# Wider zero matmuls in fewer instructions, some of them in a bank that is free

## The chip, the cores and the metric

One core of a Trainium2 chip. The time is that of one launch on the device, in microseconds (us). A ratio is the mean time of one kernel's fast runs over that of the other's of the same rounds, so not quite the ratio of the medians quoted beside it.

## The reference, cut to what matters

A recurrent attention (retention with a decay per head: 4 batches, 8 heads, 768 positions, head size 64), then a feed-forward layer on its output, all in float32:

```python
state = gamma * state + einsum('bhd,bhe->bhde', k[:, :, t], v[:, :, t])
y[:, :, t] = scale * einsum('bhd,bhde->bhe', q[:, :, t], state)
...
h = x @ w_in          # 3072 x 512 times 512 x 2048
g = h - np.tanh(h)
out = g @ w_out
```

The weights arrive as float64; the kernel loads them as raw words and converts them itself, tile by tile.

## The kernel before

The attention goes in chunks of 128 positions. A bank is here the tile that a product of TensorE is written to; the program frees it when another engine has read it (the zeros ahead of `t4` wait 1.47 us for VectorE before they may write theirs). Long before the last chunk is done, the up and down products of the feed-forward layer begin. The opening is scheduled by hand, in a string of pieces, each a letter and a number. What this document needs of them, for chunk n:

- `L` loads k, q and v; `t` and `T` transpose k and q on TensorE, `c` and `C` copy these out on ScalarE.
- `p` makes the products of chunk n, `m` masks them and `z` takes the state on VectorE; the bank is free after `z`.
- `b` and `r` are the first and second half of the outputs (into `y`), `e` a small read by ScalarE between them, `y` the copy of the output to `xT`, the input of the feed-forward layer.
- For weight tile n: `W` loads it, `A` begins its conversion on ScalarE, `D` goes on on VectorE, `G` ends it, mostly on GpSimd.
- `u` and `v` are the two halves of up product n; `x` asks for zeros.

```python
    idle = [0]

    def keep_busy(at):
        for _ in range(idle[0]):
            nc.tensor.matmul(at, busy, busy, start=True, stop=True, skip_group_check=True)
        idle[0] = 0
...
    order = """
    L0 x8 t0 c0 s0 x5 T0 w0 L1 C0 x3 t1 W0 p0 c1 s1 m0 x2 T1 z0 W1 C1 w1 x3 b0 p1 e0 A0 r0
    m1 z1 y0 A1 D0 L2 x4 b1 t2 e1 c2 G0 r1 s2 y1 D1 x3 T2 w2 L3 u0 C2 W2 p2 G1 s3 t3 m2 T3
    w3 c3 v0 z2 C3 b2 A2 L4 p3 e2 W3 D2 a0 r2 s4 y2 w4 q0 W4 m3 z3 G2 x9 t4 b3 A3 d0 T4 e3
    C4 r3 g0 L5 y3 x1 p4 A4 W5 u2 D3 s5 v2 W6 w5 m4 D4 u1 G3 a2 q2 z4 L6 x6 t5 d2 G4 T5 A5
    ...
    """
```

`busy` is a 128 x 128 tile of zeros. `x9 t4` notes nine zeros, and `t4` then writes them into its own bank before its transposes: TensorE is to have work while it waits; the aim is that its clock stays up.

## Time and profile before

| | us |
|---|---|
| median of the first 3 runs | 755.27 (754.33 to 755.91) |
| profiled span | 752.6 |
| TensorE busy | 739.6 |
| TensorE idle before 50 us / from 50 to 740 / after 740 | 7.2 / 1.6 / 4.2 |

The lines are in the prediction; one more of the timeline of TensorE, the zeros ahead of `t5` (start, length, instruction, records, and in brackets how long the engine had been idle and for whom):

```profile
43.56 1.58 PE L212 MATMUL kqTp<-busy 128*128 128x128 f32 x12 [0.31 <-DVE state L327]
```

From here to the end of the span are 709.0 us. TensorE is idle for 5.8 us of them, 4.2 of these after 740 us.

### The profile page before, as it was taken

How to read it: one execution, taken by the hardware profiler on the slowest of the kernel's cores; microseconds unless marked ns; L12 is line 12 of the kernel's file. 1: busy time of each engine (PE TensorE's matmuls, PEld its weight loads, DVE VectorE, ACT ScalarE, POOL GpSimd, SP SyncE). 2: the span in 40 equal slices, each digit the busy share in tenths (PEclk: the TensorE clock that was granted, in tenths of full speed). 3: DMA queues.
4: the chain of work that ended last, by engine and by line, in shares of the span. 5: the costliest groups of instructions: out<-in, count | busy, mean ns of one | idle time of the engine just before them, and what ended most of it. 6: DMA issues, size and time to landing. Idle time of an engine off the chain costs nothing.

```text
span 752.6 us, 13801 instructions
## 1 busy us (share of the span) xinstructions
PE 739.6 (98%) x5470; PEld 501.9 (67%) x5470; DVE 518.7 (69%) x807; ACT 389.1 (52%) x725; POOL 125.9 (17%) x108
## 2 busy tenths in 40 slices
PE   7899999999999999999999999999999999999997
PEld 7786666666667676766676666666666666666663
DVE  4899889998898666656565656555665566556653
ACT  3667486666665545445545545444344434433441
POOL 0564445435453111100111100000000000000000
PEclk9999999999999999999999999999999999999999
DMA  9982546556553353332442422000000000000000
GB/s 191 231 204 59 127 99 180 149 148 160 149 128 91 92 140 115 88 82 78 106 99 74 96 57 58 28 1 1 29 0 1 28 1 0 29 0 1 28 2 28
DMA packets 125392, 59.76 MB, mean 79 GB/s; under 512 B 109840, under 2 KB 118160, under 8 KB 125328
## 3 DMA queue, kind: packets, MB, share of 16 engines
q1 hardware_dynamic: 125184, 58.73, 30.5%
q8 instruction: 43, 0.70, 0.4%
q10 hardware_dynamic: 144, 0.15, 0.1%
q14 instruction: 21, 0.17, 0.1%
HBM read 35.80 MB, written 14.68 MB: 67 GB/s over the span
## 4 chain that ended last, share of the span: by engine, by line
PE 94%; DVE 2%; DMA 1%; SPq 1%; ACT 1%; issue 1%; DVEq 0%; ACTq 0%
PE h L414 43%; PE o L462 43%; PE y L352 3%; PE s L298 2%; PE s L304 1%; DMA raws<-in_moe_w_in_dram 1%; PE kqTp L250 1%; DMA k<-in_k_dram 1%; SPq L229 1%; PE kqTp L212 0%; DVE head L185 0%; PE y L212 0%; SPq L154 0%; DVE head L183 0%; DVE g L453 0%
## 5 line engine op out<-in xcount | busy, mean ns | idle before, releaser
L414 PE MATMUL h<-xT,w 128*128 128x256 f32 x1536 | 349.9, 381 | 0.3 <-DVE w L199 0.3
L462 PE MATMUL o<-w,g 128*128 128x512 f32 x768 | 345.6, 593 | 1.4 <-DVE sum L471 0.9
L414 PEld LDWEIGHTS h<-xT,w 128*128 128x128 f32 x1536 | 289.7, 190 | 71.1 <-issue 34.0
L462 PEld LDWEIGHTS o<-w,g 128*128 128x128 f32 x768 | 145.4, 190 | 145.7 <-issue 136.6
L423 ACT ACTIVATE u<-h 128x512 f32<-128x512 f32 x96 | 57.3, 597 | 292.0 <-PE h L414 291.9
L439 DVE TENSOR_TENSOR th<-h,th 128x512 f32<-128x512 f32 x96 | 66.3, 690 | 176.0 <-ACT th L424 175.9
L453 DVE COPY_PREDICATED g<-large,th 128x512 f32<-128x512 int32 x96 | 72.1, 751 | 10.6 <-ACT apart L273 0.5
L442 DVE SCALAR_TENSOR_TENSOR h<-q,h 128x512 f32<-128x512 f32 x96 | 66.9, 696 | 10.4 <-DVE h L440 0.5
L448 DVE SCALAR_TENSOR_TENSOR h<-q,h 128x512 f32<-128x512 f32 x96 | 66.8, 696 | 9.9
L431 ACT ACTIVATE q<-u,tab 128x512 f32<-128x512 f32 x96 | 69.4, 723 | 0.0
L432 ACT ACTIVATE q<-u,tab 128x512 f32<-128x512 f32 x96 | 69.0, 718 | 0.0
L433 ACT ACTIVATE large<-u,tab 128x512 f32<-128x512 f32 x96 | 68.7, 716 | 0.0
L452 DVE TENSOR_TENSOR g<-h,u 128x512 f32<-128x512 f32 x96 | 66.3, 691 | 3.3
L440 DVE SCALAR_TENSOR_TENSOR h<-u,h 128x512 f32<-128x512 f32 x96 | 65.8, 685 | 0.0
L424 ACT ACTIVATE th<-h 128x512 f32<-128x512 f32 x96 | 56.8, 591 | 0.0
L236 POOL TENSOR_TENSOR q<-q,tab 128x512 f32<-128x512 f32 x22 | 23.2, 1057 | 199.7 <-DMA q<-in_q_dram 113.5
L195 POOL TENSOR_TENSOR low<-low,power 128x512 f32<-128x512 f32 x30 | 38.7, 1290 | 102.2 <-DVE power L187 80.6
L199 POOL TENSOR_TENSOR w<-low,head 128x512 f32<-128x512 f32 x30 | 38.5, 1284 | 2.4
L352 PEld LDWEIGHTS y<-a,v 64*64 64x64 f32 x768 | 15.8, 134 | 17.2 <-ACT large L433 10.6
L236 POOL TENSOR_TENSOR v<-v,tab 128x512 f32<-128x512 f32 x22 | 26.5, 1206 | 0.2 <-DMA v<-in_v_dram 0.2
L352 PE MATMUL y<-a,v 64*64 64x64 f32 x768 | 21.1, 224 | 2.3 <-issue 1.8
L382 ACT COPY seen<-y 64x1 f32<-64x1 f32 x96 | 10.1, 154 | 25.3 <-PE y L352 24.9
(49 smaller groups left out, 374.4 us busy)
## 6 DMA issues: line engine op xcount, KB each, us to landing
rows<-apart SPq DMA_DIRECT2D x16, 512.0 KB, 2.6
k<-in_k_dram SPq DMA_DIRECT2D x24, 256.0 KB, 4.0
q<-in_q_dram SPq DMA_DIRECT2D x24, 256.0 KB, 4.9
v<-in_v_dram SPq DMA_DIRECT2D x24, 256.0 KB, 5.3
raw<-in_moe_w_out_dram SPq DMA_DIRECT2D x12, 512.0 KB, 3.5
out_dram<-sum SPq DMA_DIRECT2D x24, 256.0 KB, 2.0
raw<-in_moe_w_in_dram SPq DMA_DIRECT2D x14, 256.0 KB, 4.2
raw<-in_moe_w_in_dram SPq DMA_DIRECT2D x28, 128.0 KB, 3.9
```

The source lines that it names most:

```text
L352: nc.tensor.matmul(y[ds(D * col, D), r, p // 2, ts(a, D)], lhsT, rhs, start=start, stop=True, skip_group_check=True)
L414: nc.tensor.matmul(hp, w1[:, c, ts(2 * m2 + i, P)], xT[n // 2][:, c, ts(n % 2, TH)], start=(i == 0 and c == 0), stop=(c == NC - 1), skip_g ...
L431: nc.scalar.activation(q0, u, AF.Square, bias=bias0)
L432: nc.scalar.activation(q1, u, AF.Square, bias=bias1, scale=math.sqrt(A))
L433: nc.scalar.activation(large, u, AF.Relu, bias=bias_m)
L439: nc.vector.tensor_tensor(th, hp, th, op=ALU.subtract)
L440: nc.vector.scalar_tensor_tensor(hp, in0=u, scalar=R, in1=hp, op0=ALU.subtract, op1=ALU.mult, reverse0=True)
L442: nc.vector.scalar_tensor_tensor(hp, in0=q0, scalar=C0, in1=hp, op0=ALU.add, op1=ALU.mult)
L448: nc.vector.scalar_tensor_tensor(hp, in0=q1, scalar=A * C1, in1=hp, op0=ALU.add, op1=ALU.mult)
L452: nc.vector.tensor_tensor(flat, hp, u, op=ALU.mult)
L453: nc.vector.copy_predicated(flat, large.bitcast(I32), th)
L462: nc.tensor.matmul(o_p[j], gT[n, m2][:, i, ts(j, P)], w2[:, 2 * m2 + i], start=(first and i == 0), stop=(last and i == 1))
```

## The change

The intent: the same number of zero columns in fewer, wider instructions, up to a bank of 512, and in three places a bank of the up product that is free (`X`), so that the zeros need not wait until the bank of the work behind them is released.

```diff
     def keep_busy(at):
-        for _ in range(idle[0]):
-            nc.tensor.matmul(at, busy, busy, start=True, stop=True, skip_group_check=True)
-        idle[0] = 0
+        most = at.shape[-1] // P
+        while idle[0]:
+            n = min(idle[0], most)
+            zeros = busy[:, None, :].to_broadcast([P, n, P])
+            nc.tensor.matmul(at[:, : n * P].rearrange("p (n t) -> p n t", n=n), busy, zeros,
+                             start=True, stop=True, skip_group_check=True)
+            idle[0] -= n
...
-        keep_busy(tp[:, :P])
+        keep_busy(tp)
...
-        keep_busy(y[:, 0, 0])
...
+        "X": lambda n: (idle.__setitem__(0, n), keep_busy(bank("h", "zeros"))),
...
-    ... C1 w1 x3 b0 ... L2 x4 b1 ... G2 x9 t4 ...
+    ... C1 w1 X3 b0 ... L2 X4 b1 ... G2 X12 t4 ...
```

The other calls of `keep_busy` get their whole bank in the same way.

More of the change, by code (lines that the diff above doesn't have):

```diff
@@ L291, in products @@
         sp = banks("t", f"s_{ci}")
-        keep_busy(sp[:, 0, :P])
+        keep_busy(sp[:, 0])
         scores[ci] = halves = sp.rearrange("p r (w n t) -> p r w n t", w=2, n=NP)
@@ L411, in up @@
         hp = hps[n, m2][:, ts(i, TH)]
-        keep_busy(hp[:, :P])
+        keep_busy(hp)
         for c in range(NC):
@@ L459, in down @@
             o_p[j] = bank("o", f"o_{n}_{m2}_{j}")
-            keep_busy(o_p[j][:, :P])
+            keep_busy(o_p[j])
         for i in range(2):
@@ L547 @@
     order = """
-    L0 x8 t0 c0 s0 x5 T0 w0 L1 C0 x3 t1 W0 p0 c1 s1 m0 x2 T1 z0 W1 C1 w1 x3 b0 p1 e0 A0 r0
-    m1 z1 y0 A1 D0 L2 x4 b1 t2 e1 c2 G0 r1 s2 y1 D1 x3 T2 w2 L3 u0 C2 W2 p2 G1 s3 t3 m2 T3
-    w3 c3 v0 z2 C3 b2 A2 L4 p3 e2 W3 D2 a0 r2 s4 y2 w4 q0 W4 m3 z3 G2 x9 t4 b3 A3 d0 T4 e3
+    L0 x8 t0 c0 s0 x5 T0 w0 L1 C0 x3 t1 W0 p0 c1 s1 m0 x2 T1 z0 W1 C1 w1 X3 b0 p1 e0 A0 r0
+    m1 z1 y0 A1 D0 L2 X4 b1 t2 e1 c2 G0 r1 s2 y1 D1 x3 T2 w2 L3 u0 C2 W2 p2 G1 s3 t3 m2 T3
+    w3 c3 v0 z2 C3 b2 A2 L4 p3 e2 W3 D2 a0 r2 s4 y2 w4 q0 W4 m3 z3 G2 X12 t4 b3 A3 d0 T4 e3
     C4 r3 g0 L5 y3 x1 p4 A4 W5 u2 D3 s5 v2 W6 w5 m4 D4 u1 G3 a2 q2 z4 L6 x6 t5 d2 G4 T5 A5
```

## The prediction

> **What bounds the kernel now.** I read the page first: busy shares, the slices, the chain that ended last.
>
> ```profile
> PE 739.6 (98%) x5470; PEld 501.9 (67%) x5470; DVE 518.7 (69%) x807; ACT 389.1 (52%) x725; POOL 125.9 (17%) x108
> ...
> PE   7899999999999999999999999999999999999997
> ...
> PE 94%; DVE 2%; DMA 1%; SPq 1%; ACT 1%; issue 1%; DVEq 0%; ACTq 0%
> ```
>
> TensorE is busy for 739.6 of 752.6 us: all idle time together is 13.0 us, 1.7% of the span. No change that only fills or removes idle time can reach 2% (15.1 us). The low slices are the first two and the last. The table of windows says where the 13 us lie: 1.6, 2.5, 1.1 and 1.7 us in the first four stretches of 10 us, 0.3 in the fifth, none from 50 to 120, 1.6 from 120 to 740, and 4.2 after 740. The change touches only pieces before about 61 us, so the waits of TensorE in the opening matter:
>
> ```profile
> PE y L352 <- issue: 1.8, 1, 1.8
> PE kqTp L212 <- DVE state L327: 1.8, 2, 1.5
> PE kqTp L212 <- DVE busy L101: 1.1, 1, 1.1
> ...
> PE y L212 <- ACT xT L393: 0.7, 1, 0.7
> PE s L212 <- ACT kqT L262: 0.6, 1, 0.6
> ...
> PE y L352 <- ACT seen L382: 0.5, 1, 0.5
> PE h L414 <- DVE w L199: 0.3, 1, 0.3
> ```
>
> L212 is the matmul of zeros. Two of these waits stand ahead of zeros that themselves need nothing but a place to write: `y` (0.7) and `kqTp` (1.5 of the 1.8). Then the timeline of TensorE (start, length, records):
>
> ```profile
> 1.05 3.70 PE L212 MATMUL kqTp<-busy 128*128 128x128 f32 x16 [1.05 <-DVE busy L101]
> ...
> 13.42 0.28 PE L352 MATMUL y<-a,v 64*64 64x64 f32 x4
> 15.48 0.45 PE L352 MATMUL y<-a,v 64*64 64x64 f32 x12 [1.78 <-issue]
> 16.61 1.16 PE L212 MATMUL y<-busy 128*128 128x128 f32 x8 [0.68 <-ACT xT L393]
> ...
> 25.19 1.99 PE L414 MATMUL h<-xT,w 128*128 128x256 f32 x8 [0.34 <-DVE w L199]
> ...
> 30.67 2.25 PE L212 MATMUL kqTp<-busy 128*128 128x128 f32 x18 [1.47 <-DVE state L327]
> ...
> 35.26 0.46 PE L352 MATMUL y<-a,v 64*64 64x64 f32 x16 [0.46 <-ACT seen L382]
> 36.30 0.49 PE L212 MATMUL s<-busy 128*128 128x128 f32 x2 [0.57 <-ACT kqT L262]
> ```
>
> A float32 matmul is two records, so x18 is nine zeros. What the reader is to see: after each place where the change can win time there is a later row in brackets where TensorE waits anyway (25.19 for VectorE's weights, 35.26 and 36.30 for ScalarE). From 43.56 us on TensorE waits no more until after 120; only time won at that point reaches the end.
>
> [...] 128 columns every 0.111 us ((0.83 - 0.275) / 5 in a group of six records), 256 every 0.216 (16 in 3.46 us at 90.33), 512 every 0.429 (8 in 3.43 us at 86.90). So four zeros of 128 cost 8 x 0.111 = 0.89 us and one of 512 costs 2 x 0.429 = 0.86. [...] The first 16 records come every 0.228 us against 0.111 later[...]; the gaps of up to 1.8 us later on did not bring the slow rate back. [...] The page of this kernel has 43 packets and 0.70 MB on such a queue, 16 KB each[...]. [...]
>
> **The change part by part.**
> (a) Wider zeros. 47 zeros (8, 5, 3, 2, 3, 4, 3, 9, 1, 6, 3) become 17 instructions of 50 units of 128 columns (12 in place of 9). Own time: 47 x 0.222 = 10.4 us before, 50 x 2 x 0.429 / 4 = 10.7 us after. No saving by itself. The zeros that remain after 43 us, x6 and x3, get cheaper by about 0.05 us together.
> (b) Fewer instructions. 30 fewer matmuls are 120 fewer instructions in the block stream. I read the unexplained 1.78 us "issue" stall at 13.7 as a block that had not arrived: a 16 KB packet is in flight from 12.7 to 14.0 while the queues are full, and about 450 instructions had gone by[...]. Ahead of that place 14 matmuls (56 instructions) go, and 12 more in the next zeros. So the second half of chunk 0's outputs (r0) gets through before the stall, ending near 13.9 rather than 15.9, and the stall falls into b1.
> (c) X4 ahead of b1, in a free bank: no wait for the copy of y0. With r0 early, that copy can start when ScalarE has done its two conversions (14.9) and end at 15.5. b1 begins near 15.6 to 15.8 rather than 17.7, a local gain of 1.9 us. But t2 needs k_2, which lands at 11.45 + 6.1 = 17.55; r1 needs ScalarE, held until 18.2 by a conversion whose weights land at 16.9; T2 needs the scaled q, which GpSimd works on from 18.71 to 19.88 because q lands at 18.6. T2 so starts at about 19.9 and not 20.41: of 1.9 us, 0.5 remain.
> (d) That 0.5 us goes through u0 to the products of chunk 2 (22.67 to 22.2), then to nothing on TensorE: v0 waits for VectorE, which is busy from 13.65 to 28.5 without a break, and starts at 25.19 again. But the load of chunk 4 waits for exactly those products (issued at 23.43), and the weights queued behind it land at 33.52 and hold ScalarE. Both move by 0.5.
> (e) X12 ahead of t4, no wait for bank t: starts at 29.2, not 30.67, and takes 3 x 0.86 = 2.57 us, not 2.09, so t4 starts at 31.8 and not 32.76: 0.95 us. Then r3 waits at 35.26 for ScalarE, which had waited until 33.52 for weights. All of the 0.95 is lost there; what counts is the 0.5 of (d).
> (f) r3, p4, the mask, VectorE's conversion, state, x6: each is released by the one before, so x6 moves from 43.56 to about 43.05.
> (g) X3 ahead of b0: the zeros there did not wait before. 0.
> Sum on the path: 0.5 + 0.05, about 0.6 us. The order of the compiled program has the waits I expect: none on the three new groups, the wait for the copy on b1, the wait for VectorE on t4, and no new wait for the up product's bank (three extra turns of that pool could have made u2 wait for VectorE's last step on u0).
>
> **Rivals.**
> A: everything won arrives: 1.9 + 0.95 us, and perhaps 0.6 at the s bank, about 3 us, 752.3. For it: TensorE is on the chain 94% of the time. Against: the waits at 25.19, 35.26 and 36.30, each for another engine or a landing.
> B: nothing arrives, 755.3: if the early weights land no earlier because the DMA engines are full (DMA share 0.9 to 1.1 through the first 40 us), or VectorE's conversion, slowed while GpSimd works beside it (1.37 us for 0.43 at 39.11), ends at the same time. Plausible; a third of my weight.
> C: the clock falls back or a new block stall appears, because the zeros run during a wait and no longer after it[...]: 1 to 4 us slower, 757 to 759. Against: gaps stay under 2 us[...].
>
> **Range and chances.** Of 755.27, 0.6 us off is 754.7. The three runs of before spread over 1.6 us, as much as the whole effect, and B or a larger part of A move it by 1 us either way: 753.5 to 755.9. With 13 us idle in all, 2% faster is practically shut out; 2% slower would need a throttled stretch of 30 us at half rate.
>
> **What would show it.** Right: the stall of kind "issue" appears later in the program, among the y matmuls of chunk 1, or is shorter; t4's zeros start near 29.2; waits for ScalarE at r3 (near 34.8) grow by some 0.4 us; the zeros after u1 (x6) start near 43.05; the work from there to the end keeps its length, 709.1 us. Wrong: x6 at 42 or earlier (then A, and the DMA landing moved more than I think), or at 43.5 or later (B); the stall at the same instruction as before would refute the block reading; zeros of 512 columns spaced more than 0.43 us, or bracketed waits ahead of the new groups, would refute (a) and (c).

Cut out of the prediction is what no trace of this case shows: rules on the spacing of matmuls, the clock and the arrival of instructions, and a count of blocks that rests on them. The sum loses no term by it: 0.5 us from (d) and 0.05 us from (a), about 0.6 us. "Such a queue" there is the line `q8 instruction: 43, 0.70, 0.4%` of the page, and a "block" is one of its packets of 16 KB. That TensorE waits for a block, and the 1 to 4 us of rival C, were estimates of mine.

## The result, and the profile after

The changed kernel takes 754.44 us (median of 6, 754.10 to 757.14), the kernel before 754.70 (median of 6, 754.06 to 755.91): ratio 1.0003, 95% interval 0.9986 to 1.0021. Nothing is won that these runs can show; a gain as small as the 0.6 us expected (a ratio of 0.9992) lies inside the interval, so the times alone cannot exclude it either.

The page of the changed kernel, TensorE's busy time and the chain that ended last:

```profile
PE 741.0 (98%) x5410; PEld 496.2 (66%) x5410; DVE 518.5 (69%) x807; ACT 388.9 (52%) x725; POOL 126.5 (17%) x108
...
PE 87%; DVE 7%; SPq 2%; DMA 1%; ACT 1%; issue 1%; DVEq 0%; ACTq 0%
```

60 records fewer, yet TensorE is busy 1.4 us longer, and VectorE has 7% of the chain where it had 2%. The waits of TensorE, longest in total first:

```profile
PE kqTp L256 <- DMA k<-in_k_dram: 1.9, 2, 1.6
PE y L357 <- ACT seen L387: 1.5, 2, 1.2
...
PE kqTp L217 <- DVE state L333: 0.6, 1, 0.6
PE s L217 <- ACT kqT L268: 0.6, 1, 0.6
```

The waits of zeros for `y` and the stall called "issue" are gone; a wait for a load of k and a longer one for ScalarE have come. The timeline of TensorE shows where (L217 is the zeros, L357 the outputs, L256 the transposes):

```profile
13.43 0.44 PE L357 MATMUL y<-a,v 64*64 64x64 f32 x16
13.80 1.12 PE L217 MATMUL zeros<-busy 128*128 128x512 f32 x2
14.97 0.69 PE L357 MATMUL y<-kqT,state 64*64 64x64 f32 x32
...
17.47 0.66 PE L256 MATMUL kqTp<-tab,k 128*128 128x128 f32 x4 [1.56 <-DMA k<-in_k_dram]
...
19.08 1.65 PE L217 MATMUL kqTp<-busy 128*128 128x384 f32 x2
...
29.26 2.84 PE L217 MATMUL zeros<-busy 128*128 128x512 f32 x6
...
35.14 0.46 PE L357 MATMUL y<-a,v 64*64 64x64 f32 x16 [1.16 <-ACT seen L387]
...
43.78 1.53 PE L217 MATMUL kqTp<-busy 128*128 128x512 f32 x4 [0.65 <-DVE state L333]
```

Read it from the top. `r0` (13.43) runs through without the stall. `b1` starts at 14.97 instead of 17.70, 2.7 us early. Then TensorE stands for 1.56 us for the keys of chunk 2. The zeros at 19.08 take 1.65 us where a group of this width takes 0.81 elsewhere in the trace. The new zeros at 29.26 start without the 1.47 us of wait, and the transposes behind them start at 31.93 instead of 32.76; 1.16 us of wait for ScalarE follow. At 43.78, the zeros ahead of `t5` are 0.2 us later than before, after a longer wait for VectorE.

Why the slow zeros? The table of windows (busy time of each engine, then the granted clock) over three stretches of the changed kernel:

```profile
15.00:18.30 3.30, 1.56 (x52) 1.18 (x52) 3.06 (x7) 1.47 (x6) 0.00 (x0) 1.00 0.84 162
18.30:21.70 3.40, 3.26 (x23) 2.38 (x24) 3.30 (x5) 1.35 (x5) 2.51 (x2) 0.51 1.11 227
```

The clock falls to half, 0.51 over 3.4 us. In the kernel before it is 1.00 in the same stretches, with TensorE busy for 2.14 us in the first. Being early had made TensorE idle (1.56 busy of 3.30 us), and then the clock fell: the very thing that the zeros are meant to prevent.

The length of the gap alone does not decide it. Run both_after below has a longer gap at this place, 2.17 us against 1.56, and its profiled run a mean clock of 1.0, where that of the changed kernel has 0.997. What does decide it was not shown. Nor does the clock fall so far in every run of the changed kernel: three of the six have a mean clock of 0.999 or 1.000, the others 0.995 to 0.998.

### The profile page after: what moved, and what is told of

It reads as the page before. It is cut to its first block, busy times and chain, and to the rows that moved or that the text cites. A ratio compares the mean times of both kernels' runs of the same rounds, so it can differ in the third digit from the quotient of the medians.

```text
span 752.8 us, 13681 instructions
## 1 busy us (share of the span) xinstructions
PE 741.0 (98%) x5410; PEld 496.2 (66%) x5410; DVE 518.5 (69%) x807; ACT 388.9 (52%) x725; POOL 126.5 (17%) x108
## 4 chain that ended last, share of the span: by engine, by line
PE 87%; DVE 7%; SPq 2%; DMA 1%; ACT 1%; issue 1%; DVEq 0%; ACTq 0%
PE h L419 40%; PE o L467 40%; PE y L357 3%; PE s L304 1%; PE s L310 1%; SPq L235 1%; DVE head L185 1%; DMA raw<-in_moe_w_in_dram 1%; DVE h L453 1%; DVE g L457 1%; SPq L154 1%; DVE head L183 1%; DVE h L447 1%; DVE th L444 1%; DMA raws<-in_moe_w_in_dram 1%
## 5 line engine op out<-in xcount | busy, mean ns | idle before, releaser
L357 PEld LDWEIGHTS y<-a,v 64*64 64x64 f32 x768 | 15.8, 136 | 16.3 <-ACT large L438 10.6
L357 PE MATMUL y<-a,v 64*64 64x64 f32 x768 | 21.1, 226 | 1.5 <-ACT seen L387 1.5
```

What stands on the lines that cost most here:

```text
L357: nc.tensor.matmul(y[ds(D * col, D), r, p // 2, ts(a, D)], lhsT, rhs, start=start, stop=True, skip_group_check=True)
```

## The experiments

All twelve gave the reference's result. Diffs are against the changed kernel unless said otherwise. Two theories. **Clock**: the gain that should have come through was spent in the half-clock stretch; fill the gap and it comes back. **Bound elsewhere**: `t5` waits for a chain of DMA, ScalarE and VectorE that doesn't care when TensorE gets its early work done; then full clock wins nothing either, and the gain appears only when that chain is shortened. The start of the zeros ahead of `t5` is the gauge: what follows is about 709.0 us in every trace, so the gauge tells the span to 0.1 us except where noted.

| run | second outputs of chunk 3 | tile 3 of the weights landed | zeros ahead of t5 | rest | span | median us |
|---|---|---|---|---|---|---|
| before | 35.26 | 33.52 | 43.56 | 709.0 | 752.6 | 754.70 |
| changed | 35.14 | 33.43 | 43.78 | 709.0 | 752.8 | 754.44 |
| wide_old | 35.42 | 33.68 | 43.79 | 709.0 | 752.8 | 754.38 |
| narrow_new | 35.79 | 34.07 | 44.23 | 709.1 | 753.3 | 755.20 |
| fill_gap | 35.25 | 33.55 | 44.73 | 709.1 | 753.8 | 754.57 |
| x9_in_t | 34.61 | 32.48 | 43.17 | 709.0 | 752.2 | 754.35 |
| late_convert | 33.84 | 32.64 | 44.31 | 709.1 | 753.4 | 755.15 |
| early_state | 35.29 | 33.59 | 43.12 | 709.0 | 752.1 | 754.61 |
| both_after | 35.39 | 34.35 | 43.44 | 709.7 | 753.1 | 753.26 |
| both_after_again | 34.04 | 32.04 | 42.08 | 709.1 | 751.2 | 753.14 |
| both_before | 37.16 | 34.41 | 45.20 | 709.0 | 754.2 | 753.86 |
| weights_first | 33.77 | 28.24 | 41.70 | 709.4 | 751.1 | 753.48 |
| weights_first_before | 34.67 | 27.67 | 42.60 | 709.0 | 751.6 | 753.39 |
| early_state_before | 35.11 | 31.76 | 43.04 | 709.1 | 752.1 | 753.84 |

(Times in the trace of the profiled execution, from its start; "rest" is the span less the gauge; the landing is that of the last of the tile's three transfers. The median is over all runs of a kernel, and the profiled one is not always typical: in both_before and fill_gap its span, 754.2 and 753.8 us, is longer than that of most of the kernel's other runs, 752.0 to 752.1 and 752.3 to 752.8. Beside the experiments the kernel before had 11 runs, median 755.28.)

**1. wide_old: the wide zeros alone, places and numbers as before.**

```diff
-        begun = set()
+        keep_busy(y[:, 0, 0])
+        begun = set()
-        most = at.shape[-1] // P
+        most = max(1, at.shape[-1] // P)
-    ... X3 b0 ... X4 b1 ... X12 t4 ...
+    ... x3 b0 ... x4 b1 ... x9 t4 ...
```

> Wide zeros alone: each group of zeros back at its old place, with its old number and its old bank (the two groups into the y banks stay 128 wide, for the slice has no more). If the 1.78 us stall at 13.7 us was a block of instructions that had not arrived, it is gone from r0 here too (48 fewer instructions ahead of it), and chunk 1's outputs start near 16 us. If the stall has another cause, it is back at r0. Theory 'clock': the gap ahead of t2 is shorter (about 0.7 us, as the y zeros now wait for the copy and run later), so the clock falls less often than in the changed kernel; the zeros ahead of t5 start at 43.0 to 43.6. Total within 0.1% of both kernels.

Measured: 754.38 us, ratio 0.9992 (0.9979 to 1.0004). The second half of chunk 0's outputs ran in one piece from 13.33 us, without the stall; chunk 1's began at 15.96 and the gap ahead of `t2` was 0.16 us. The clock stayed full. The gauge stood at 43.79. So fewer instructions alone remove the stall, and without any fall of the clock nothing arrives either. What was unexpected: `u0` and the products behind it were 0.8 us early, the load of chunk 4 was issued at 22.61 us instead of 23.43, and tile 3 of the weights, queued behind it, landed no earlier (33.68).

**2. narrow_new: new places, narrow zeros.**

```diff
-        most = at.shape[-1] // P
+        most = 1
```

> New places and the new numbers, but every zero 128 columns wide, so the instruction count ahead of r0 is that of the kernel before. Block reading: the stall of about 1.8 us stands inside r0 again, ending near 15.5 us. Chunk 1's outputs then start near 16.9 us (zeros run while the copy of y is awaited). Little idle time is left ahead of t2 (k lands near 17.5), so theory 'clock' expects full clock through 45 us and T2 near 19.9, p2 near 22.2, the zeros ahead of t5 near 43.1; the rival (VectorE and the landings hold the end whatever the clock does) expects 43.5 to 43.8.

Measured: 755.20 us, ratio 1.0007 (0.9994 to 1.0020). The stall is back, at the same instruction as before. The timeline:

```profile
13.58 0.28 PE L357 MATMUL y<-a,v 64*64 64x64 f32 x4
14.41 0.45 PE L357 MATMUL y<-a,v 64*64 64x64 f32 x12 [0.54 <-issue]
```

Four records, a pause, twelve records: the same split as in the kernel before (there 1.78 us). All four kernels with narrow zeros in the experiments and the kernel before it have it, for 0.54 to 1.78 us; none of the nine with wide zeros has. The pause stands at the same instruction in all five traces: four records of `r0`, a pause, twelve (in the trace of the kernel before, 445 matmuls and weight loads start ahead of it). A second pause of 0.74 us came at 33.4 us. The pause is shorter here than the 1.8 us expected, and a packet of the instruction queue came earlier: the 16 KB one before the pause ended at 12.89 us here and at 14.00 in the kernel before, and TensorE went on 1.52 and 1.48 us later; in all six pauses it is 1.43 to 1.65 us. That the pause lasts until that packet's instructions are there fits this, but is my reading: no run varied the arrival of a packet by itself. The gauge, 44.23, followed the landing of tile 3 (34.07).

**3. fill_gap: nine more zeros in the two gaps of the changed kernel.**

```diff
-    ... X4 b1 t2 e1 c2 ...
+    ... X4 b1 X7 t2 X2 e1 c2 ...
```

> The changed kernel with seven more zeros ahead of t2 and two ahead of r1, in the free bank of the up product: they fill the 1.56 us and 0.32 us gaps in which TensorE waited. Theory 'clock': no half-clock stretch in the records (mean granted clock back to 0.9996 or 1.000 in every run), T2 near 19.9 and the products of chunk 2 near 22.2 us instead of 23.4, chunk 4's load issued near 22.9 instead of 24.1, zeros ahead of t5 near 43.1 us, total 0.5 us under the kernel before, and less spread between runs. Rival: clock full, but the zeros ahead of t5 still start at 43.5 to 43.8 and nothing is won.

Measured: 754.57 us, ratio 0.9999 (0.9987 to 1.0012). The timeline of TensorE:

```profile
15.75 1.77 PE L217 MATMUL zeros<-busy 128*128 128x512 f32 x4
...
25.19 1.99 PE L419 MATMUL h<-xT,w 128*128 128x256 f32 x8 [1.15 <-DVE w L199]
...
44.73 1.53 PE L217 MATMUL kqTp<-busy 128*128 128x512 f32 x4 [1.49 <-DVE state L333]
```

The gap is filled, the clock is full, `T2` is at 19.54 and the load of chunk 4 at 22.61, 1.5 us earlier than in the changed kernel. All as "clock" expected up to here, and then the gain is gone twice: 1.15 us at `v0`, which waits for weights from VectorE and starts at 25.19, to the hundredth as before; and 1.49 us at the gauge, which is the latest but one of all. Theory "clock" falls as the reason for the missing gain: in every one of the fourteen traces, fast clock or slow, `v0` starts between 25.09 and 25.44 us. (The late gauge is that of the profiled run, 755.54 us; the interval alone would leave room for the 0.5 us expected.) One of its five runs still had a clock of 0.998.

**4. x9_in_t: the zeros ahead of t4 put back behind the wait for their bank.**

```diff
-    ... G2 X12 t4 ...
+    ... G2 x9 t4 ...
```

> The changed kernel with the zeros ahead of t4 put back: nine of them, in the transposes' own bank, behind its release. If the 0.9 us that the new place wins at t4 is lost in the wait for ScalarE at r3 (as 1.16 us of wait there suggest), t4 starts near 32.8, r3's wait shrinks to 0.3 to 0.5 us, r3 starts at 35.1 as before, and the total and the zeros ahead of t5 (43.6 to 43.8) do not change. If t4 were on the path, r3 and everything after moves later by 0.9 us.

Measured: 754.35 us, ratio 0.9998 (0.9984 to 1.0011).

```profile
30.59 2.18 PE L217 MATMUL kqTp<-busy 128*128 128x512 f32 x6 [1.47 <-DVE state L333]
32.60 0.60 PE L256 MATMUL kqTp<-tab,k 128*128 128x128 f32 x4
...
34.61 0.46 PE L357 MATMUL y<-a,v 64*64 64x64 f32 x16
```

`t4` starts 0.67 us later than in the changed kernel and nothing comes later: in this profile tile 3 landed 1 us sooner, so the second outputs even started 0.5 us sooner, with no wait at all. So the test is not a clean one: the early landing removed the wait for ScalarE in which the 0.67 us would have been lost. The total tells of no worth of the new place in this schedule.

**What holds the end.** In the six rows of the table where tile 3 landed later than 33 us and ScalarE's order is that of the kernel before (before, changed, wide_old, narrow_new, fill_gap, early_state), the second outputs of chunk 3 start 1.70 to 1.74 us after the landing. In between ScalarE, in order, converts the tile (1.2 us) and reads `y`. Behind them come the products of chunk 4, their mask, the conversion of tile 4 and only then the state on VectorE. The timeline of VectorE in the kernel before, one kind of instruction on two tiles, and the state:

```profile
35.25 0.43 DVE L183 TENSOR_SCALAR head<-head 128x512 uint32<-128x512 uint32 x1
...
39.11 1.37 DVE L183 TENSOR_SCALAR head<-head 128x512 uint32<-128x512 uint32 x1
...
42.54 0.42 DVE L323 TENSOR_TENSOR state<-s,state 128x256 f32<-128x256 f32 x1
```

0.43 us while GpSimd is idle, 1.37 us while it is at work (from 36.75 to 41.61): four instructions that took 2.1 us for tile 3 take 4.1 for tile 4, ahead of a state that needs none of them.

**5. late_convert: tile 3's conversion behind ScalarE's copies.**

```diff
-    ... X12 t4 b3 A3 d0 T4 e3 C4 r3 ...
+    ... X12 t4 b3 d0 T4 e3 C4 A3 r3 ...
```

> The changed kernel with ScalarE's first conversion of weight tile 3 moved behind the copy of chunk 4's transposes, so that the landing of that weight (33.5 us) no longer holds the second half of chunk 3's outputs. If the landing is what ate the 0.95 us won at t4: the wait at 35.14 for ScalarE (1.16 us) shrinks to about 0.2, those outputs start near 34.0 and the products of chunk 4 near 35.3 instead of 36.6. But VectorE must still convert tiles 3 and 4 before chunk 4's state, so the zeros ahead of t5 stay at 43.3 to 44.0 and their wait for VectorE grows from 0.65 to 1.5 to 2 us; total unchanged within 0.5 us.

Measured: 755.15 us, ratio 1.0013 (0.9999 to 1.0027).

```profile
33.84 0.46 PE L357 MATMUL y<-a,v 64*64 64x64 f32 x16
...
44.31 1.53 PE L217 MATMUL kqTp<-busy 128*128 128x512 f32 x4 [2.27 <-DVE state L333]
```

As expected: the landing lets go, the outputs start 1.3 us earlier, and the whole of it and more is waited out for VectorE.

**6. early_state: the state ahead of tile 4's conversion on VectorE.**

```diff
-    ... w5 m4 D4 u1 G3 a2 q2 z4 L6 x6 t5 ...
+    ... w5 m4 z4 D4 u1 G3 a2 q2 L6 x6 t5 ...
```

> The changed kernel with chunk 4's state taken ahead of the conversion of weight tile 4 on VectorE (the state needs nothing of it). If VectorE's conversion, slowed beside GpSimd, is what holds the zeros ahead of t5 at 43.8 us, their wait (0.65 us) goes and they start as soon as the last up product is done, near 43.1 us; the total falls by the same 0.5 to 0.65 us, and the rest of the span stays 709.0 us. If the wait stays, something else holds them.

Measured: 754.61 us (752.66 to 757.02), ratio 0.9995 (0.9974 to 1.0016).

```profile
43.12 1.45 PE L217 MATMUL kqTp<-busy 128*128 128x512 f32 x4
```

No wait, and the start expected. The profiled span falls by 0.7 us. The runs as a whole are unclear: three with a granted clock of 1.0 took 752.66, 752.67 and 754.00 us, three with 0.998 or less took 755.22 to 757.02.

**7 and 8. both_after, both_after_again: both edits.**

> Both edits on the changed kernel. Neither the landing nor VectorE's conversion holds TensorE then: zeros ahead of t5 near 41.6 to 42.0 us instead of 43.8. If they were the two bounds that hid the change, the total falls by 1 to 2 us, to about 753; VectorE is busy without a break from 43 to 92 us, so part may be given back there and the rest of the span may grow from 709.0 to 710.

> The kernel of both_after once more, since its profiled execution had one late weight (VectorE 2 us behind) and its zeros ahead of t5 at 43.4 while four of its five executions were 1.6 us faster. An undisturbed profile should show them near 41.6 to 42.0 and a total of 753.0 to 753.4; ratio to the kernel before again near 0.998.

Measured: first 753.26 us, ratio 0.9980 (0.9968 to 0.9993); again 753.14 us, ratio 0.9975 (0.9962 to 0.9988). In the first profile the weights of tile 2 came 3 us late (28.24 us) and VectorE with them. It also has the gap that kept its clock; the mean clock of this run is 1.0:

```profile
17.11 0.69 PE L357 MATMUL y<-kqT,state 64*64 64x64 f32 x32 [2.17 <-ACT xT L398]
```

The second profile is undisturbed:

```profile
34.04 0.46 PE L357 MATMUL y<-a,v 64*64 64x64 f32 x16
...
42.08 1.45 PE L217 MATMUL kqTp<-busy 128*128 128x512 f32 x4
```

1.7 us before the changed kernel. The two edits together beat both kernels: the slowest run of the second five, 753.34 us, is below the fastest that either had (754.06).

**9. both_before: the same two edits on the kernel before.**

> The same two edits on the kernel before (narrow zeros, old places): tells what the change is worth once its bounds are lifted. There t4 starts 0.8 to 0.95 us later than in the changed kernel; so zeros ahead of t5 near 42.6 to 43.0 and a total 0.5 to 1 us above the changed kernel with both edits. If instead it equals that kernel, the change is worth nothing even when TensorE sets the pace.

Measured: 753.86 us, ratio 0.9992 (0.9977 to 1.0006), a gauge of 45.20 in the profile. The zeros ahead of `t4` in the timeline, then a line of the table of windows, whose last figure but two is the clock:

```profile
31.43 3.87 PE L212 MATMUL kqTp<-busy 128*128 128x128 f32 x18 [2.18 <-DVE state L327]
```

```profile
31.70:35.10 3.40, 3.40 (x18) 3.40 (x18) 3.05 (x6) 0.38 (x1) 1.61 (x2) 0.52 0.88 234
```

Here TensorE waited 2.18 us ahead of its zeros, the clock was 0.52 in the 3.4 us from 31.70, and the zeros themselves ran at little more than half the rate (18 records in 3.87 us, against 2.25 in the kernel before) and pushed `t4` to 35.15 us. That is the case for which a free bank is made. The expected size of the difference to the changed kernel with these edits (0.5 to 1 us) fits the medians, but the interval doesn't settle it.

**10 and 11. weights_first, weights_first_before: early state, and tile 3 loaded ahead of chunk 4.**

```diff
-    ... A2 L4 p3 e2 W3 D2 ... m4 D4 u1 ... z4 L6 ...
+    ... A2 W3 L4 p3 e2 D2 ... m4 z4 D4 u1 ... L6 ...
```

> The changed kernel with chunk 4's state ahead of the conversion of weight tile 4 (as in early_state), and weight tile 3 loaded ahead of chunk 4 instead of behind it, so that its load is issued near 21.7 us instead of 26.7. If the landing of that tile holds ScalarE until 33.5, ScalarE's conversion of it starts by about 31 to 32, the wait of 1.3 us at chunk 3's second outputs is gone (they start near 33.9), the products of chunk 4 near 35.2 instead of 36.7, and the zeros ahead of t5 near 41.8 instead of 43.1; total 1 us under early_state's undisturbed runs (752.7), near 752 to 752.5. Rival: chunk 4's keys, now later in the queue, hold t4 instead, and nothing is won.

> The same two edits on the kernel before. With landing and conversion out of the way TensorE sets the pace, and its zeros ahead of t4 wait for the transposes' bank: t4 about 0.9 us later than in the changed kernel with these edits, zeros ahead of t5 about 0.8 us later, total 0.5 to 1 us more. If both come out alike, the new places are worth nothing even then.

Measured: on the changed kernel 753.48 us, ratio 0.9983 (0.9971 to 0.9996); on the kernel before 753.39 us, ratio 0.9981 (0.9967 to 0.9995). Neither the 752 to 752.5 us expected of the first nor a difference of 0.5 to 1 us between the two came. First the timeline of the changed kernel with these edits, then that of the kernel before with them:

```profile
33.77 0.46 PE L357 MATMUL y<-a,v 64*64 64x64 f32 x16
...
41.70 1.45 PE L217 MATMUL kqTp<-busy 128*128 128x512 f32 x4
```

```profile
30.57 2.25 PE L212 MATMUL kqTp<-busy 128*128 128x128 f32 x18 [1.47 <-DVE state L327]
...
42.60 1.50 PE L212 MATMUL kqTp<-busy 128*128 128x128 f32 x12
```

Tile 3 lands at 28.24 us and ScalarE waits no more for it. The gauge differs by 0.90 us, just what the place of the zeros wins at `t4` (31.76 against 32.66). So in the traces the mechanism of the change is real once TensorE sets the pace. But the rest of the span is 709.4 us against 709.0, so 0.5 us is left in the span, and the medians don't show even that; in the pair of both edits (runs 7 to 9) they differ by 0.6 to 0.7 us. What the change is worth then stays open.

**12. early_state_before: the early state on the kernel before.**

> Only the earlier state on the kernel before. Its zeros ahead of t5 waited 0.31 us for VectorE, so they start near 43.25 instead of 43.56; the total falls by 0.3 us in undisturbed runs, as low as 753.9 against 754.1 to 754.4 for the kernel before, and stays 0 to 0.5 us above early_state's undisturbed runs.

Measured: 753.84 us (753.69 to 753.90), ratio 0.9984 (0.9971 to 0.9998). The gauge is at 43.04 without a wait; tile 3 had landed early, at 31.76 us. The ratio is 1.2 us off, four times the 0.3 us expected; the gauge accounts for 0.5 us, part of it from the early landing, and the rest was not traced. Nor do these runs lie within 0.5 us of early_state's two fastest (752.66 and 752.67). The least edit of all comes near the ratios that the larger ones reach on the changed kernel (0.9975 to 0.9983); why was not found.

## Why the prediction was right or wrong

The measured time lies in the range, and "within 2%" was right for the reason given: 13 us idle in all. That 754.44 lies so close to the 754.7 expected is luck: the step was taken from 755.27, and the kernel before came out at 754.70 itself. The 0.6 us expected did not show.

- (a) Wider zeros cost nothing and win nothing: nearly so. Twelve zeros took 2.67 us wide (29.26 to 31.93) and 2.78 narrow (29.26 to 32.04). Inside the group the wide records came every 0.429 us, as priced; only the first took longer, 0.533 us, which the price had left out (a narrow one takes 0.213 there).
- (b) The stall as a block of instructions that had not arrived: it stood at the same instruction in every narrow kernel and in no wide one, and its end followed an instruction packet by 1.43 to 1.65 us. Both fit the block reading; that TensorE waits for the packet was not shown by itself. The pause was expected to reappear later, inside b1; it did not, and so `b1` won 2.7 us and not 1.9. In the changed kernel the packet ended at 13.29 us, so the block was there by about 14.9 (an estimate from the six pauses: 1.65 us later), and TensorE had started as many matmuls and weight loads (445) at 15.20.
- (c) Most of that lost to landings ahead of `t2` and `T2`: right, but its price was missed. After the idle time the clock was 0.51 for 3.4 us, and `T2` came at 20.52 instead of 19.9. Rival C had named the clock and I had dismissed it with "gaps stay under 2 us"; this gap was 1.56 us, and the clock fell behind it.
- (d) The step that failed. "The load of chunk 4 waits for exactly those products ... and the weights queued behind it land at 33.52 ... Both move by 0.5." In the changed kernel the load was later (24.14 against 23.43), because of the slow clock (0.51 from 18.3 to 21.7 us). Where it did move, in wide_old and fill_gap by 0.8 us, the landing did not: 33.68 and 33.55. Issued between 22.55 and 22.74 us in eight profiles, that load was followed by landings of tile 3 between 31.76 and 34.41. That the DMA engines' load decides it is my guess (their share is 1.00 from 28 to 35 us in the changed kernel); it was not tried apart from the order of issue.
- (e) The 0.95 us at `t4` lost at the wait for ScalarE: right, though 0.83 us was won and not 0.95: 1.16 us of wait, and x9_in_t lost nothing by giving it up.
- (f) "Each is released by the one before": right as a chain, but with (d) gone there was nothing to hand on. VectorE's conversion of tile 4, slowed beside GpSimd, ended it at 43 us; early_state shows that it held `t5`.
- (g) No wait, no gain: right.

In the profiled run rival B is what happened: the gauge stands at 43.78, past the 43.5 us that was to tell of it. The times cannot tell B from a gain of 0.6 us. Taken at a clock of 0.999 or more alone, three runs of the changed kernel average 754.18 us against 754.75 for six of the kernel before, but these were picked afterwards and come from other rounds, so they show nothing yet.

The spread between runs goes in part with the granted clock, which I had not in mind: of the 11 runs of the kernel before beside the experiments, six had a clock of 0.999 or more and took 754.75 us on average, five had 0.997 or 0.998 and took 755.73.

## What to carry to other kernels

Work done sooner on the busiest engine is worth only what the next wait leaves of it: follow it to the point after which that engine waits no more, and compare that one start. Look for work that stands in an engine's order ahead of something urgent and isn't needed by it; moving one such piece of VectorE's work here did more than the rearranged zeros (early_state_before 0.9984, the change 1.0003). And filler that is meant to keep a clock up should not itself wait for a buffer (in both_before it waited 2.18 us and the clock was 0.52 behind that); here the free bank showed at the gauge only where TensorE set the pace (0.90 us between weights_first_before and weights_first, nothing in x9_in_t).
